# A scheduled DeltaNet + SwiGLU kernel: a planner that counts TensorE's instruction packets, weight buffers let go one by one, and a new order

## The chip, the cores and the metric

The kernel runs on one core of one Trainium2 chip. The metric is device time in microseconds (us) of one execution. Before the change three runs took 669.87, 666.66 and 668.11 us (median 668.11). A separate execution was profiled; it took 668.94 us.

## The reference

Two blocks follow each other. DeltaNet runs over 4 batches x 8 heads x 768 steps with head dimension 48; its output, rearranged to 3072 tokens of 384 values, goes through an RMS norm and a SwiGLU feed-forward with 1536 hidden columns. All in float32.

```python
k_n = k / (np.linalg.norm(k, axis=-1, keepdims=True) + 1e-06)
for t in range(S):
    kt, vt, bt = (k_n[:, :, t], v[:, :, t], beta[:, :, t, None])
    y[:, :, t] = np.einsum('bhd,bhde->bhe', q[:, :, t], state)
    v_old = np.einsum('bhde,bhd->bhe', state, kt)
    state = state + bt[:, :, :, None] * np.einsum('bhd,bhe->bhde', kt, vt - v_old)
...
x = np.ascontiguousarray(attn_out.transpose(0, 2, 1, 3)).reshape(B * S, H * D)
...
rms = np.sqrt(np.mean(x * x, axis=-1, keepdims=True) + 1e-06)
xn = x / rms * rms_g
g = xn @ w_gate
silu = g * (1.0 / (1.0 + np.exp(-g)))
val = xn @ w_val
return (silu * val @ w_out).astype(np.float32)
```

## The kernel before

**Tiling.** The 768 steps are cut into 12 chunks of 64. For each chunk, `prep` makes the triangular inverse that turns the step-by-step recurrence into matmuls (chunks 0 and 1 by `invert`, the others by a sequence of VectorE or GpSimd operations and DMAs), `qpart` makes the masked scores, `recur` applies the state, makes the chunk's output, normalizes it and updates the state, and `ffn` or `ffn_plain` runs the feed-forward of the chunk's 256 tokens. Chunks 0 and 1 use `ffn_plain`: `up` (line 1331, six matmul instructions for each side, gate or value, of a 128-column block) and `down_mm` (L1313). The other chunks use a scheme with fewer products: `ffn` (L1426) and `down` (L1483).

**Small matmuls.** The recurrence uses matmuls of 64 rows and columns or less, 64 instructions and 64 weight loads an operation: L563 (scores), L675, L782 and L801 (`invert`), L1037 and L1052 (on the state), L1100, L1114, L1134, L1171 (`recur`). They follow each other far more densely than those of the feed-forward. L1259 transposes the normalized output of a chunk, and L1264, L1268 scale it into the feed-forward's input x. Filler matmuls (L1594) pad TensorE's waits in the start-up.

**The order.** Every operation is first put on a list by `P.add`, with its engine, an estimated duration, keys that it reads and writes, PSUM groups that it takes and gives back, and `size`, the number of instructions that it puts on TensorE's stream (a float32 matmul is two weight loads and two matmul instructions). There are 2,790. `Plan.run` decodes the string `ORDER`, two characters an operation, into one order of all of them; each engine's queue is that order restricted to the engine (SP's queue issues most DMAs). `Plan.times` walks the order and gives each operation a planned start. The planned starts are not used as times on the chip; they decide which PSUM bank a group gets (the one that by plan is free first) and where and how many filler matmuls are put, up to 110 us by plan. In `times`, TensorE's instruction fetch is modelled as a backlog: a store that fills at a constant rate (`FETCH`, `AHEAD`).

**Weights and the hold.** The weight matrices arrive as 18 transfers of 768 KB (64-bit numbers, converted on the chip). `weights` issues them from SP into seven `raw` buffers, and each is converted by two ScalarE and two VectorE operations (L475, L476, L470, L473). The first four go out at once. `hold` (line 490) makes the buffers raw[4], raw[5] and raw[6] wait: one tiny GpSimd copy into each reads `u_`, chunk 0's result of L1145, so that their transfers start only then. On SP's queue a transfer that waits keeps back all that follow it.

**The start-up.** The k of chunk 0 comes in two halves, one issued by SP, one by ScalarE. TensorE transposes it (`turn`, L540), ScalarE squares it (L584), VectorE sums (L585, L587), GpSimd takes the root (L589), VectorE goes on (L592 and the following). Then `invert` for chunk 0 is a serial chain, followed by `recur(0)` up to x at L1268, and the feed-forward of chunk 0 begins. `betas` (L643) needs two small loads of beta.

Of the kernel before, what the change touches and what calls it, by code (L numbers as in the profile page):

```python
# [9 lines left out]
FP32 = mybir.dt.float32  # L10
# [6 lines left out]
C = 64  # L17
W = 32
# [3 lines left out]
FETCH, AHEAD = 67.0, 120.0  # L22
EARLY, FETCH0, AHEAD0 = 130.0, 50.0, 150.0
# [9 lines left out]
    "#.#'#&#3#)#4###,#-#(#/#*#0#T#C#`#W#>#^#a#_#w#U#X#k#Y#$#Z#d#l#b#n#m#o#c#H#t#V#e#+#u#f#[#]#q#v#x#s#R#y#S#@#z#M#p#{#1#|"  # L33
    "#?#2#}#E#i#~#j$C$#${$$#r$'$($%$&$)$*#N$D$/#J$.#D$+$0$1$,$H#I%$$E#=$2$F$-%)#K$7$5#L$3$8$6$<#O#h#A$=$>$;$4$9#P$G$?%V$:"
    "#g$I$B#F$L$K$J$i$l$O$N$M#B$P$Q$R&2%Y$[$S$@#G$T$]%W%Z$^$V$k$j$U$_$v%X$f$q%e$`$a$W$m$b$Y%[$c$d#Q$X$Z$e$n$o&Q$A&E%]%`%^"
    "$|&F$p%a$~$w&I%_&G%b$x&H&J$y$s%3%c$r&M%d$g%.&K$t&N$h&3&L$z#5&R&O%f$}$u'2%g%+&4&P%h'3%%%#&S'4&+%i%&&,&T%j%*%=%k&X%8%l"
    "&U%/%B%,&Y&V(4%1%m(5&^%n&Z%0#8&_&-#7&[%q%G%r%o%2&W%4%s%p&]&`%x%5%6%y%L&.#:%t%z%C#<&/&a%{%u%7&0%v%-%D'-%w%}%~%|%'%(&c"
    "&#&1%:#%&5&d'Q%H'0%9&b&?%E%?%Q%F'T'a%J'R&''.%I'1&&&@%K&$&('S&7%;&)'U&%#6'/%>'V&*&e%@'5%A'W'X%<'8%R'Y&h':'[%T%S&f'Z'9"
    "(6&i']%U&8'7%M&6&m'6&j(7%N&g(8'^)-#9).(<'K(9&k):#;';);%O&r'<%P'_&s&9'=)/'?&n)0'>(:'L&l)n'M&o&t&p'b&u&q'@'`'N)q'A'c)o"
    "'B&:&w'P)r'd'e)p'O'f'C&v'g'h'G'i)s'j&x&A)u'k*P'H&|&C&y'l'D'E'F)t&{'m'I'J)y&z&})w'n&B)v'o'$&~*Q'#)x'p'%&D'q(;(I'r's'&"  # L40
# [75 lines left out]
class Plan:  # L116
# [90 lines left out]
    def run(self, free, filler=None, until=0.0):  # L207
# [1422 lines left out]
```

## Time and profile before

| | us |
|---|---|
| median of three runs | 668.11 (666.66 to 669.87) |
| the profiled execution, its time | 668.94 |
| the profiled execution, its span | 667.2 |
| ScalarE busy | 295.7 |
| GpSimd busy | 133.7 |

How to read what follows: times are us from the span's start. A row of the timeline has the start, the length, the engine, the line, the instruction, what it writes and reads, the shapes, a count, and in brackets the idle time before it and what ended it ("issue" means that nothing visible was waited for). PE is TensorE's matmuls, PEld its weight loads, DVE VectorE, ACT ScalarE, POOL GpSimd, SP SyncE; a q behind the name is the engine's queue issuing a DMA. In a view of stretches, each row has the stretch, its length, then for PE, PEld, DVE, ACT and POOL the busy time and the number of instructions, then the granted TensorE clock, the DMA engines' busy share and GB/s.

### The profile page before, as it was taken

The page shows a single profiled execution, that of the slowest core. Times are in us where ns is not written, and L with a number is a line of the kernel's source. Part 1 is how long each engine was busy: PE and PEld are TensorE (multiplying, and loading weights), DVE is VectorE, ACT ScalarE, POOL GpSimd, SP SyncE. Part 2 cuts the span into 40 slices and gives each one's busy share as a digit, 9 for nine tenths or more (in the row PEclk, how much of TensorE's full clock was granted, in tenths as well). Part 3 has the DMA queues.
Part 4 walks back from the last instruction along what each step waited for, and adds up shares of the span by engine and source line. Part 5 has one row for each costly group of instructions (what it writes and reads, how often), then busy time and mean ns, then how long its engine had stood idle before and what let it go on. Part 6 is the DMA issues. An engine that isn't in the chain of part 4 may idle for free.

```text
span 667.2 us, 23209 instructions
## 1 busy us (share of the span) xinstructions
PE 654.4 (98%) x9934; PEld 604.8 (91%) x9934; DVE 543.3 (81%) x1147; ACT 295.7 (44%) x705; POOL 133.7 (20%) x204
## 2 busy tenths in 40 slices
PE   9999999999999999999999999999999999999997
PEld 5687887887799999999999999999999999999997
DVE  5879799888898798799888898799898799557463
ACT  4677553235336435454445345344445244263240
POOL 2210423021610410520410410420410301000000
PEclk9999899999999999999999999999999999999999
DMA  9959754666465566376375565666355333300101
GB/s 213 239 157 269 203 140 72 109 160 103 64 113 78 118 106 127 68 136 102 68 126 98 88 113 108 111 114 114 73 98 103 74 63 67 63 31 20 25 1 25
DMA packets 270423, 69.36 MB, mean 104 GB/s; under 512 B 257456, under 2 KB 262576, under 8 KB 270000
## 3 DMA queue, kind: packets, MB, share of 16 engines
q1 hardware_dynamic: 269280, 67.68, 51.1%
q8 instruction: 78, 1.28, 0.8%
q10 hardware_dynamic: 1040, 0.20, 0.2%
q14 instruction: 25, 0.20, 0.1%
HBM read 49.76 MB, written 22.02 MB: 108 GB/s over the span
## 4 chain that ended last, share of the span: by engine, by line
PE 91%; DVE 3%; issue 2%; POOL 2%; SPq 1%; DMA 1%; ACT 0%; POOLq 0%; ACTq 0%
PE bank L1426 40%; PE bank L1483 19%; PE bank L1331 8%; PE bank L1313 4%; PE bank L563 3%; PE bank L1037 3%; PE bank L1594 3%; PE bank L1114 2%; PE bank L1100 1%; PE bank L782 1%; PE bank L801 1%; PE bank L1171 1%; PE bank L979 1%; PE bank L999 1%; SPq L377 1%
## 5 line engine op out<-in xcount | busy, mean ns | idle before, releaser
L1426 PE MATMUL bank<-xf,w_in 128*128 128x128 f32 x1440 | 178.8, 276 | 0.3 <-DVE tmp L1436 0.3
L1426 PEld LDWEIGHTS bank<-xf,w_in 128*128 128x128 f32 x1440 | 169.3, 192 | 1.8 <-DVE tmp L1436 0.5
L1436 DVE TENSOR_TENSOR tmp<-tmp,bank 128x512 f32<-128x512 f32 x180 | 120.1, 682 | 46.9 <-PE bank L1426 28.9
L1426 PE MATMUL bank<-xf,more 128*128 128x128 f32 x960 | 122.8, 276 | 0.1
L1426 PEld LDWEIGHTS bank<-xf,more 128*128 128x128 f32 x960 | 114.9, 192 | 1.3 <-DVE tmp L1436 0.3
L1438 ACT COPY tmp<-bank 128x512 f32<-128x512 f32 x120 | 68.5, 587 | 99.9 <-PE bank L1426 78.5
L930 DVE TENSOR_REDUCE acc<-acc 128x30 f32<-128x90 f32 (+4 forms) x150 | 71.0, 473 | 5.2
L1442 ACT ACTIVATE tmp<-tmp 128x256 f32<-128x256 f32 x120 | 47.6, 415 | 61.9 <-DVE tmp L1436 61.8
L1483 PE MATMUL bank<-wo_sb,hf 128*128 128x192 f32 x360 | 64.0, 329 | 0.0
L1483 PEld LDWEIGHTS bank<-wo_sb,hf 128*128 128x128 f32 x360 | 58.0, 190 | 1.1 <-issue 0.4
L924 DVE TENSOR_TENSOR acc<-acc,at 128x60 f32<-128x60 f32 (+4 forms) x150 | 52.9, 353 | 5.9 <-POOL at L904 2.8
L1443 DVE TENSOR_TENSOR hf<-tmp 128x256 f32<-128x256 f32 x120 | 47.7, 418 | 3.0 <-ACT tmp L1442 2.2
L608 POOL TENSOR_TENSOR knrm<-ksum,half 128x16 f32<-128x16 f32 x11 | 32.0, 2913 | 85.2 <-DVE ksum L587 85.1
L869 POOL TENSOR_TENSOR at<-at,beta_b 128x256 f32<-128x256 f32 (+3 forms) x32 | 18.0, 593 | 149.0 <-DMA at<-dkk 149.0
L1313 PE MATMUL bank<-wo_sb,hf 128*128 128x384 f32 x96 | 33.8, 488 | 1.1 <-issue 1.1
L1331 PE MATMUL bank<-xp,w_in 128*128 128x256 f32 x144 | 34.7, 397 | 0.1
L1331 PE MATMUL bank<-xf,w_in 128*128 128x256 f32 x144 | 33.0, 382 | 0.0
L1331 PEld LDWEIGHTS bank<-xp,w_in 128*128 128x128 f32 x144 | 28.0, 198 | 4.5 <-DVE hf L1340 0.2
L1283 DVE TENSOR_TENSOR xf<-xf 128x256 f32<-128x256 f32 (+1 forms) x70 | 27.5, 432 | 5.2 <-ACT xf L1253 2.6
L1331 PEld LDWEIGHTS bank<-xf,w_in 128*128 128x128 f32 x144 | 26.9, 190 | 4.5
L950 POOL COPY acc<-acc 128x128 f32<-128x128 f32 x40 | 16.3, 438 | 71.4 <-DVE acc L930 70.7
L1313 PEld LDWEIGHTS bank<-wo_sb,hf 128*128 128x128 f32 x96 | 17.8, 190 | 10.3 <-issue 1.3
(207 smaller groups left out, 989.4 us busy)
## 6 DMA issues: line engine op xcount, KB each, us to landing
at<-dkk SPq DMA_DIRECT2D x20, 256.0 KB, 4.3
vt<-in_v_dram SPq DMA_DIRECT2D x24, 192.0 KB, 4.4
out_dram<-tmp SPq DMA_DIRECT2D x48, 96.0 KB, 2.2
k<-in_k_dram SPq DMA_DIRECT2D x23, 192.0 KB, 4.7
dks<-k SPq DMA_DIRECT2D x14, 256.0 KB, 4.0
kt<-dks SPq DMA_DIRECT2D x28, 128.0 KB, 3.8
more<-in_moe_w_gate_dram SPq DMA_DIRECT2D x4, 768.0 KB
more<-in_moe_w_out_dram SPq DMA_DIRECT2D x4, 768.0 KB
```

What stands on the lines that cost most here:

```text
L608: P.add("POOL", 2.95, lambda: nc.gpsimd.tensor_tensor(out=knrm[i2], in0=ksum[i2], in1=half, op=ALU.pow), pn, r=[("ksum", i2), "half"], w=[ ...
L924: nc.vector.tensor_tensor(out=acc[:, 1:3, 0:n, j + 2 : W].rearrange("p a i t -> p i a t"), in0=acc[:, old, 0:n, j : j + 2, None].to_broadc ...
L930: nc.vector.tensor_reduce(out=acc[:, new, 0:n, j + 2 : W], in_=acc[:, lo : lo + 3, 0:n, j + 2 : W].rearrange("p a i t -> p i t a"), axis=A ...
L1283: P.add("DVE", V(128 * n), lambda dst=dst, a=a, b_=b_, op=op: nc.vector.tensor_tensor(out=dst, in0=a, in1=b_, op=op), pxv, r=[("xp", 0), ( ...
L1313: nc.tensor.matmul(po[p].t[:, 0:DM], hf[:, spot(f), 128 * p : 128 * p + 128], wo_sb[:, spot(f)], start=(f == f0), stop=(f == f1 - 1), skip ...
L1331: nc.tensor.matmul(ps.t[:, TOK * side : TOK * side + TOK], w_in[:, side, h_, 3 * t + i_, n : n + 128], x_[:, 2 * t : 2 * t + 2].rearrange( ...
L1426: nc.tensor.matmul(g.t[:, 128 * z : 128 * z + 128], fac[:, side, 128 * f : 128 * f + 128], xf[:, xs], start=(begin and z == 0), stop=False ...
L1436: P.add("DVE", V(512), lambda t=t, g=g: nc.vector.tensor_tensor(out=t, in0=t, in1=g.t, op=ALU.add), -1, r=[g], w=[tk], last=g)
L1438: P.add("ACT", A(512), lambda t=t, g=g: nc.scalar.copy(t, g.t), -1, r=[g], w=[tk], last=g)
L1442: P.add("ACT", A(256), lambda t=t: nc.scalar.activation(out=t[:, 0:256], in_=t[:, 0:256], func=ACTF.Silu), -1, w=[tk])
L1443: P.add("DVE", V(256), lambda t=t, f0=f0, p=p: nc.vector.tensor_tensor(out=hf[:, spot(f0) : spot(f0) + 2, 128 * p : 128 * p + 128], in0=t[ ...
L1483: nc.tensor.matmul(g.t[:, 0:192], a_[:, f], b_[:, f], start=(begin and f == 0), stop=(f == 5), skip_group_check=True)
```

## The change

Three edits. First, `Plan.times` no longer models a backlog but packets: a packet of instructions is asked for whenever the count of instructions passes `PACKET[0] + PACKET[1] * n`, is there after `LAG[0]` plus a share of the DMA server's backlog, and TensorE waits for it when the count reaches its need, `PACKET[2]` instructions after the asking. The number of fillers is now worked out there too (`op.fill`), and `run` uses it. Second, `hold` has three different reads: raw[4] still waits for `u_`, raw[5] for the first tile of chunk 0's mean square and root (`ms[0]`), raw[6] for chunk 0's x (`xp1`). Third, `ORDER` is another permutation of the same 2,790 operations; it differs from the first line of the string to nearly the last. No computing operation is added or taken away.

```diff
-FETCH, AHEAD = 67.0, 120.0
-EARLY, FETCH0, AHEAD0 = 130.0, 50.0, 150.0
+PACKET = (130.2, 254.45, 314.0)
+LAG = (4.2, 0.55, 7.0)
...
 ORDER = (
-    "#.#'#&#3#)#4###,#-#(#/#*#0#T#C#`#W#>#^#a#_#w#U#X#k#Y#$#Z#d#l#b#n#m#o#c#H#t#V#e#+#u#f#[#]#q#v#x#s#R#y#S#@#z#M#p#{#1#|"
...
+    "#.#'#-###3#)#4#&#(#$#/#*#0#>#`#W#C#^#a#T#_#X#k#2#,#w#Y#b#Z#l#d#n#m#c#o#U#t#e#H#V#f#u#+#[#]#v#E#x#s#y#z#M#?#{#j#q#|#1"
...
-        server, self.end, mode, backlog, lands = 0.0, 0.0, 0, 0.0, []
+        server, self.end, mode, lands = 0.0, 0.0, 0, []
+        first, each, reach = PACKET
+        count, asked, used, there, pe = 0, 0, 0, {}, 0.0
+        lag = lambda t: LAG[0] + LAG[1] * min(max(server - t, 0.0), LAG[2])
...
-                rate, store = (FETCH, AHEAD) if s > EARLY else (FETCH0, AHEAD0)
-                fill = 6.0 if s < until else 0.0
-                backlog = max(0.0, backlog - (rate - fill) * (s - at["PE"])) + op.size - rate * op.dur
-                late = max(0.0, backlog - store) / rate
-                backlog, end = max(0.0, backlog - rate * late), end + late
+                op.fill = []
+                if s < until and any(x == SPARE and s < SPARE or x <= pe for x in free):
+                    op.fill = fillers(pe, s)
+                pe = s + op.dur
+                count += 4 * len(op.fill)
+                while first + each * asked <= count:
+                    there[asked] = s + lag(s)
+                    asked += 1
+                more, late, long = count + op.size, 0.0, end - s
+                while True:
+                    a, b = first + each * asked, first + each * used + reach
+                    if a >= more and b >= more:
+                        break
+                    if a <= b:
+                        t = s + late + (long * (a - count) / op.size if op.size else 0.0)
+                        there[asked] = t + lag(t)
+                        asked += 1
+                    else:
+                        t = s + late + (long * (b - count) / op.size if b > count else 0.0)
+                        if used < asked and there[used] > t:
+                            late += there[used] - t
+                        used += 1
+                count, end = more, end + late
...
-                if s < until and spare:
-                    filler(fillers(pe, s), spare[-1][1])
+                if op.fill:
+                    filler(op.fill, spare[-1][1])
...
     def hold():
-        for n in range(HELD, 7):
-            t = raw[n].bitcast(FP32)[:, 0:1]
-            P.add("POOL", 0.15, lambda t=t: nc.gpsimd.tensor_copy(out=t, in_=u_[:, 0, 0:1]), 29, r=[("u", 0, 0)], w=[("raw", n)])
+        for n, t, key in ((HELD, u_[:, 0], ("u", 0, 0)), (HELD + 1, ms[0][:, 0], ("ms", 0, 0)), (HELD + 2, xp1[:, 0], ("x1", 0))):
+            out_, in_ = raw[n].bitcast(FP32)[:, 0:1], t[:, 0:1]
+            P.add("POOL", 0.15, lambda out_=out_, in_=in_: nc.gpsimd.tensor_copy(out=out_, in_=in_), 29, r=[key], w=[("raw", n)])
```

94 lines of the change are left out of this document (47 added, 47 removed).

## Prediction

> **What bounds the kernel now.** I read the profile's page first (busy time, the span in slices, the chain of waits, the DMA queues).
>
> ```profile
> span 667.2 us, 23209 instructions
> PE 654.4 (98%) x9934; PEld 604.8 (91%) x9934; DVE 543.3 (81%) x1147; ACT 295.7 (44%) x705; POOL 133.7 (20%) x204
> PE   9999999999999999999999999999999999999997
> q8 instruction: 78, 1.28, 0.8%
> PE 91%; DVE 3%; issue 2%; POOL 2%; SPq 1%; DMA 1%; ACT 0%; POOLq 0%; ACTq 0%
> ```
>
> TensorE is busy in every slice and carries 91% of the chain that ends last. The change adds and removes no matmul of the computation, so it can win only two things: a TensorE start that comes earlier, and holes in its stream. The timeline of TensorE splits the span.
>
> ```profile
> 1.42 4.42 PE L1594 MATMUL bank<-ident 128*128 128x512 f32 x6 [1.42 <-POOL ident masks.py:199]
> 7.18 1.04 PE L540 MATMUL bank<-ident,k 128*128 128x128 f32 x8
> 23.66 2.06 PE L782 MATMUL bank<-mt,m1bd 64*64 64x32 f32 x64
> 44.33 0.27 PE L675 MATMUL bank<-kt 64*64 64x64 f32 x1 [0.93 <-issue]
> 44.53 8.04 PE L1331 MATMUL bank<-xp,w_in 128*128 128x256 f32 x36
> ```
>
> Up to 44.53 a serial start-up runs (filler matmuls of line 1594 pad it); from 44.53 on real work is packed, 622.7 us of it. The page shows 2% "issue" in the chain: time in which TensorE waited for nothing visible. I looked for where, listing the stalls and counting instructions up to each (stretches from zero; the x after PE and PEld are matmuls and weight loads), and then two stretches around one stall.
>
> ```profile
> 0.00:29.14 29.14, 27.72 (x350) 18.24 (x350) 20.70 (x64) 16.18 (x40) 6.13 (x11) 1.00 0.93 217
> 0.00:35.10 35.10, 32.98 (x476) 22.79 (x476) 25.30 (x75) 18.41 (x44) 8.82 (x12) 1.00 0.87 215
> 0.00:43.40 43.40, 40.62 (x731) 29.65 (x731) 29.73 (x86) 23.79 (x62) 11.59 (x19) 1.00 0.82 208
> 0.00:71.15 71.15, 67.28 (x1113) 52.03 (x1114) 55.74 (x146) 44.07 (x98) 14.48 (x20) 1.00 0.84 213
> 0.00:84.80 84.80, 79.69 (x1367) 62.77 (x1368) 65.75 (x165) 53.18 (x111) 18.98 (x25) 0.98 0.80 213
> 0.00:171.20 171.20, 165.39 (x2636) 131.12 (x2637) 143.22 (x323) 87.68 (x201) 39.17 (x47) 0.99 0.72 167
> 0.00:265.60 265.60, 258.75 (x4165) 219.58 (x4165) 223.97 (x492) 129.51 (x301) 62.28 (x84) 0.99 0.65 142
> 70.33:73.75 3.42, 2.11 (x100) 2.04 (x94) 3.32 (x9) 1.46 (x2) 0.84 (x1) 1.00 0.46 88
> 73.75:77.17 3.42, 3.42 (x11) 2.75 (x10) 2.31 (x5) 2.56 (x4) 3.13 (x3) 0.50 1.02 390
> ```
>
> Adding both columns, the stalls stand at instruction 700, 952, 1462, 2227, 2735, 5273 and 8330. The steps are 252, 510, 765, 508, 2538 and 3057: 1, 2, 3, 2, 10 and 12 times about 254.5. And 19,868 TensorE instructions by 78 packets of queue 8 are 254.7 a packet. So these holes are TensorE waiting for its next packet of instructions. The diff's constants say the same: with a packet asked for at 130.2 + 254.45 n and needed 314 later, the needs fall at 699, 953, 1462, 2225, 2734, 5279, 8332, within 6 of my counts.
>
> **Part 1, the packets.** The rows of the stalls, what one of them did to the clock (12 matmuls at 73.80 beside 12 normal ones), the two small groups ahead of it, and the largest stall for data:
>
> ```profile
> 29.77 0.41 PE L782 MATMUL bank<-mt,m1bd 64*64 64x32 f32 x6 [0.63 <-issue]
> 66.51 2.06 PE L782 MATMUL bank<-mt,m1bd 64*64 64x32 f32 x64
> 68.39 1.97 PE L801 MATMUL bank<-kk,x2bd 64*64 64x32 f32 x61
> 72.39 0.50 PE L1052 MATMUL bank<-state,kt 48*64 48x48 f32 x20 [1.31 <-issue]
> 73.80 4.50 PE L1331 MATMUL bank<-xp,w_in 128*128 128x256 f32 x12
> 84.90 1.19 PEld L1134 LDWEIGHTS bank<-r,mt 64*64 64x64 f32 x38 [0.23 <-issue]
> 103.08 0.62 PE L1259 MATMUL bank<-ident,yn 128*128 128x128 f32 x3 [0.57 <-ACT yn L1241]
> 106.35 2.86 PE L1331 MATMUL bank<-xp,w_in 128*128 128x256 f32 x12
> 172.24 2.74 PE L1313 MATMUL bank<-wo_sb,hf 128*128 128x384 f32 x8 [1.06 <-issue]
> 266.26 0.30 PE L999 MATMUL bank<-x2bd,kk 128*32 128x128 f32 x1 [0.67 <-issue]
> ```
>
> After 44.53 the packet stalls cost 1.31 + 0.23 + 1.06 + 0.67 = 3.27. The stretch with the 1.31 stall is busy 2.11 of 3.42, and in the next one the granted clock is 0.50: 12 matmuls take 4.50 instead of 2.86, another 1.64. Together **4.91 us** hang on packets.
>
> Does the new order remove them? I decoded both ORDER strings (two characters an operation) and added up instructions. Between asking and need lie 314 instructions, 157 matmuls. At the 71 us stall these are 41 of line 1052, all 64 of L801 and 52 of L782, the densest kind (64 in about 1 us): from 66.8 to 71.08, 4.2 us, and the packet came 1.31 later, after 5.5. With the median spacing of each kind the other stalled intervals are 3.8 (need 4.0) and 3.7 (need 4.4); the one at 171 is 6.9 and needed nearly 8, the DMA engines being loaded. In the new order the same boundary has three operations of L1331 (18 matmuls, 3.9 us at the 1.3 for six that 106.35 shows) among the small ones and lasts 7.3; the others become 5.6, 5.0 and 6.6. The shortest after the start are 5.0, 5.0, 5.3 and 5.4, where today they are 3.7, 3.8, 4.0 and 4.6. Today eleven intervals between 4.6 and 6.3 passed without a stall. So the 4.91 go; the 6.6 one, and any that meets a full DMA, may stall again. Bounds: 0 to 4.91 given back; I take 0.6, half of one stall of today's size, nearest to those eleven intervals without one. The diff does not show how many filler matmuls the new plan puts into the start-up (its times set that, and the banks); I keep today's. Twelve instructions fewer would make the shortest interval 4.1 (the one that stalls at 265 today), twelve more leave it at 5.0.
>
> [...]
>
> **Part 2, the start.** SP's and the other queues' first rows:
>
> ```profile
> 0.79 1.64 SPq L377 DMA_DIRECT2D tmp<-in_beta_dram  x2
> 2.47 0.67 SPq L377 DMA_DIRECT2D k<-in_k_dram  x1
> 6.39 0.84 ACT L584 ACTIVATE r<-k 128x768 f32<-128x768 f32 x1 [3.34 <-DMA k<-in_k_dram]
> 9.13 0.92 DVE L585 TENSOR_REDUCE ksum<-r 128x16 f32<-128x768 f32 x1
> 10.34 3.02 POOL L589 TENSOR_TENSOR knrm<-ksum,half 128x16 f32<-128x16 f32 x1 [8.97 <-DVE ksum L587]
> 13.74 0.21 DVE L592 TENSOR_SCALAR knrm<-knrm 128x16 f32<-128x16 f32 x1
> ```
>
> The new SP order issues k's half ahead of the two beta loads: 2.47 − 0.79 = 1.68 earlier. The betas move behind two transposes on TensorE. The first transposes then need not wait for k (landing about 6.39 − 1.68 = 4.7) but for the first fillers (end 1.42 + 4.42 = 5.84), so 7.3 becomes 5.84, 1.5 earlier. VectorE's reduce is put ahead of a memset, but still follows the copy out of those transposes, and its successors follow: 9.13 becomes about 7.0 to 7.9, the power on GpSimd starts about 9.3 and VectorE goes on at 12.3 instead of 13.74: **1.4 us** for the serial chain behind it. Bounds: 0 (an unmoved load, weights or v, ends last) to 1.68.
>
> At the end of the start-up:
>
> ```profile
> 38.59 1.19 POOL L1221 TENSOR_TENSOR rs<-ms,mhalf 128x1 f32<-128x1 f32 x1 [1.70 <-DVE ms L1214]
> 39.95 0.57 SPq L377 DMA_DIRECT2D wsum<-in_moe_w_val_dram  x1
> 41.82 0.92 ACT L475 ACTIVATE xf<-hf 128x768 f32<-128x768 f32 x1 [0.78 <-DMA hf<-in_moe_w_out_dram]
> 42.64 1.14 ACT L1268 ACTIVATE xp<-bank,g_sb 128x128 f32<-128x128 f32 x4
> 46.98 0.92 ACT L475 ACTIVATE xf<-wsum 128x768 f32<-128x768 f32 x1
> ```
>
> The weight conversion at 41.82 moves behind the four scalings of L1268, so x is ready about 1 us sooner than 43.78; the k scaling on GpSimd (L819) moves behind the first hold copy and fits into the 1.70 of idle time ahead of the root at 38.59. But the stall of 0.93 ends at 44.33, and the first feed-forward matmul is past instruction 1462: that packet, not x, opens the feed-forward. I credit 0.3 (bounds 0 and 0.93). The hold copies now wait for u, the first root and x, so the transfer issued at 39.95 and what is queued behind it on SP go at about 41 to 42, 1 to 2 us later. What it carries is first used by the eleventh feed-forward operation of TensorE, ten operations of about 1.3 us after the start, so not before 56. Today a transfer into that tile was in use 7 us after its issue (46.98), which makes 49, and the conversion is four operations of under 1 us on ScalarE and VectorE: some 3 us of cover are left, and I cost it at nothing. If that cover is gone, each us late is a us.
>
> **Part 3, the rest of the order.** By the decoded strings 1,870 of 2,790 operations stand at another place on their engine, after the start mostly swaps of near neighbours. The largest stall of TensorE for data is the 0.57 at 103.08; I take the new order's stalls for data as equal to the old one's. Bounds: 0.57 won, or 4 lost (seven such stalls).
>
> **Sum**, against the profiled execution's own 668.94: −4.91 + 0.6 − 1.4 − 0.3 = −6.0, so 662.9 (span 661.2). That execution lies 0.83 above the median of 668.11; −6.0 from the median is 662.1. I forecast **662.5**.
>
> **Rivals.**
> 1. *The stalls move.* Today's long wait (8 us) came with a loaded DMA; the new order's intervals are 5 to 7. Three such hits of 1.2 and one half-clock stretch of 1.64 return 5.2: 667. For: the 390 GB/s beside 73.75; against: eleven quiet intervals. Chance 0.17.
> 2. *The start does not move* (another load ends last), the stalls go: 668.11 − 4.3 = 663.8 or a little above. Chance 0.11.
> 3. *The holes are not fetches* but sit at those operations, and stay: only the start is won, 666.4. The counted steps of 254.5 speak against it. Chance 0.04. [...]
> 4. *Slower: x of chunk 1 comes late.* The old order has seven feed-forward operations of chunk 0 between the first transposition of L1259 (103.08) and the first of chunk 1, about 1.3 us each; the new one has three, and places the transposition 4.7 us of TensorE work later, so TensorE arrives at the same absolute time with less in reserve. On GpSimd two memsets, 1.0 and 0.7 us by the plan's durations, now stand ahead of the root that releases it. Being d late costs d, and beyond about 1.3 us also a half-clock 1.64. It is slower than now from d = 4.0, and by over 0.5% from 7.3: d = 9 gives 662.5 + 9 + 1.64 = 673. For: VectorE has 81% to do and the 0.57 wait there already; against: 1.7 on GpSimd is all I can count. Chance 0.10.
>
> **Numbers.** Forecast 0.58, rivals 0.17, 0.11, 0.04, 0.10. A measurement here can tell about 0.5%, 3.3 us, from nothing. Faster by that (under 664.8): 0.57 of the forecast's chance and about half of rival 2: 0.63. Same: rivals 1 and 3, the rest of 2, and a little of 4's small end: 0.28. Slower: 0.09. Range 659.5 (all 4.91, start 1.68 + 0.93, the 0.57, and 0.5 for runs that differ) to 668.5 (rivals 1 and 3 inside).
>
> **What would show it.** Right: no stall ended by "issue" at 60 to 90, 171 and 265; granted clock 1.00 from 60 to 80; first L540 near 5.9; line 1331 starting at 42.5 to 43.3; the last TensorE work some 6 us earlier. Wrong: "issue" stalls at other multiples of 254.5 (rival 1), L1331 still at 44.5 (rival 2), idle TensorE of some us ahead of L1259 near 102 with a half clock after it (rival 4).

## The result, and the profile after

The changed kernel takes 665.38 us in the median of 9 runs (664.39 to 667.44), the kernel before 668.11 in as many on the same chip (665.57 to 670.58): a ratio of 0.9957 with a 95% interval of 0.9938 to 0.9976. It is faster by 2.7 us; forecast were 5.6. Line numbers of the changed kernel are those of before plus 21 (L1331 is now L1352, L540 L561, L782 L803, L801 L822, L675 L696, L1134 L1155, L1313 L1334, L475 and L476 L496 and L497, L473 L494, L793 L814).

From the page of the changed kernel: its span, the engines' busy time and the chain that ended last.

```profile
span 663.7 us, 23214 instructions
PE 651.1 (98%) x9922; PEld 601.6 (91%) x9922; DVE 545.8 (82%) x1147; ACT 296.7 (45%) x705; POOL 135.0 (20%) x204
PE 66%; SPq 3%; DVE 2%; DMA 1%; issue 1%; ACT 1%; DVEq 0%; ACTq 0%
```

The span is 3.5 shorter (667.2 to 663.7). There are 12 matmul records fewer, and all of them are start-up fillers: the trace shows 40 on L1615 where 52 stood on L1594. Next TensorE's timeline of the changed kernel, the rows that answer to those shown of before (start, time from there to the end of the group, what it is, and in brackets the idle time ahead of it and what ended it):

```profile
5.65 1.06 PE L561 MATMUL bank<-ident,k 128*128 128x128 f32 x8
21.95 2.06 PE L803 MATMUL bank<-mt,m1bd 64*64 64x32 f32 x64 [0.34 <-DVE mt L782]
40.56 5.45 PE L1352 MATMUL bank<-xp,w_in 128*128 128x256 f32 x24 [0.41 <-ACT xp L1289]
48.60 1.13 PE L1352 MATMUL bank<-xp,w_in 128*128 128x256 f32 x4 [0.87 <-DVE w_in L494]
75.64 1.06 PE L561 MATMUL bank<-ident,k 128*128 128x128 f32 x8 [2.48 <-issue]
84.42 1.25 PE L1155 MATMUL bank<-r,mt 64*64 64x48 f32 x36 [1.08 <-issue]
```

Read against before: the feed-forward opens at 40.56 instead of 44.53, 3.97 earlier. It is opened by x now (L1289), not by a packet. The stalls at 171 and 265 are gone. But between 47 and 85 new ones stand: 0.87, 2.48 and 1.08 us. Two of them are ended by "issue", as the packet stalls of before were. Counting instructions up to each, and looking at the clock behind the first, in stretches of the changed kernel (PE busy and matmuls, PEld busy and weight loads, VectorE, ScalarE, GpSimd, granted clock, DMA share, GB/s):

```profile
0.00:73.17 73.17, 69.14 (x1200) 53.76 (x1200) 59.48 (x154) 46.22 (x100) 16.84 (x22) 1.00 0.90 224
0.00:83.50 83.50, 76.84 (x1368) 59.84 (x1368) 67.08 (x167) 53.83 (x112) 20.61 (x26) 0.98 0.84 216
73.43:76.84 3.41, 1.20 (x9) 1.13 (x10) 1.77 (x5) 3.33 (x6) 0.83 (x1) 1.00 0.27 92
76.84:80.26 3.42, 3.42 (x30) 1.99 (x28) 2.94 (x5) 3.37 (x5) 1.08 (x1) 0.50 0.39 123
```

The stall at 83.1 stands at 1368 + 1368 = 2736 instructions: 444.2 + 9 x 254.45 = 2734, the need of packet 9. The one at 73.2 stands at 2400, some 80 short of the next need (2480): it is no packet. After it the granted clock is 0.50 for 3.42 us, which costs about 1.5: four matmuls of L1334 take 2.47, where the same four take 1.45 or 1.46 at full clock, and L822 takes 2.57 where it takes 2.06 in a run below.

What does the 2.48 us stall wait for? ScalarE's timeline of the changed kernel shows it:

```profile
73.51 0.89 ACT L496 ACTIVATE kk<-wsum 128x768 f32<-128x768 f32 x1 [1.00 <-DMA wsum<-in_moe_w_val_dram]
74.31 0.87 ACT L497 ACTIVATE tmp<-more 128x768 uint32<-128x768 uint32 x1
75.08 0.47 ACT L814 ACTIVATE kk<-bank,side 128x256 f32<-128x256 f32 x1
```

L561 starts at 75.64, 0.09 after the first L814 has let go of its PSUM bank (75.08 + 0.47). L814's own inputs came from TensorE's L803, done by 73.2; but in the new order it stands behind two weight conversions on ScalarE, and the first of these waits for a transfer that landed near 73.5. In the old order the first L814 (there L793) came ahead of it, as ScalarE's timeline of before shows:

```profile
73.91 0.47 ACT L793 ACTIVATE kk<-bank,side 128x256 f32<-128x256 f32 x1 [2.12 <-PE bank L782]
75.89 0.90 ACT L475 ACTIVATE kk<-wsum 128x768 f32<-128x768 f32 x1 [0.71 <-DMA wsum<-in_moe_w_val_dram]
```

So the account of the span is: start 3.97 won; the packet stalls and the half clock behind them 4.91 won; lost 0.87 + 2.48 + 1.5 + 1.08 = 5.9; and 0.5 won over the rest makes the 3.5. (The wait of 0.57 for yn at 103 in before is gone too: nothing stands ahead of L1280, the line of L1259, in the changed kernel.) This is the account of one profiled execution of each kernel; a second pair follows below.

### The profile page after: what moved, and what is told of

Read it like the earlier page. It is cut to its first block, busy times and chain, and to the rows that moved or that the text cites. A ratio compares the mean times of both kernels' runs of the same rounds, so it can differ in the third digit from the quotient of the medians.

```text
span 663.7 us, 23214 instructions
## 1 busy us (share of the span) xinstructions
PE 651.1 (98%) x9922; PEld 601.6 (91%) x9922; DVE 545.8 (82%) x1147; ACT 296.7 (45%) x705; POOL 135.0 (20%) x204
## 4 chain that ended last, share of the span: by engine, by line
PE 66%; SPq 3%; DVE 2%; DMA 1%; issue 1%; ACT 1%; DVEq 0%; ACTq 0%
PE bank L1447 38%; PE bank L1504 19%; SPq L398 3%; PE bank L1058 2%; PE bank L584 2%; PE bank L1121 1%; PE bank L1135 1%; PE bank L1192 1%; DMA out_dram<-tmp 1%; PE bank L1000 1%; PE bank L1020 1%; DVE xf L1304 1%; DVE tmp L1457 0%; DMA k<-in_k_dram 0%; DVE acc L945 0%
## 5 line engine op out<-in xcount | busy, mean ns | idle before, releaser
L1464 DVE TENSOR_TENSOR hf<-tmp 128x256 f32<-128x256 f32 x120 | 47.7, 418 | 5.7 <-ACT tmp L1463 5.2
L1334 PE MATMUL bank<-wo_sb,hf 128*128 128x384 f32 x96 | 35.2, 501 | 0.0
L1352 PE MATMUL bank<-xp,w_in 128*128 128x256 f32 x144 | 33.5, 383 | 1.3 <-DVE w_in L494 0.9
L1352 PE MATMUL bank<-xf,w_in 128*128 128x256 f32 x144 | 33.2, 383 | 0.0
L1352 PEld LDWEIGHTS bank<-xp,w_in 128*128 128x128 f32 x144 | 26.8, 190 | 6.2 <-DVE w_in L494 1.3
L1304 DVE TENSOR_TENSOR xf<-xf 128x256 f32<-128x256 f32 (+1 forms) x70 | 29.1, 451 | 3.7 <-ACT xf L1274 2.0
L1352 PEld LDWEIGHTS bank<-xf,w_in 128*128 128x128 f32 x144 | 26.9, 190 | 4.7 <-DVE acc L945 0.2
L1334 PEld LDWEIGHTS bank<-wo_sb,hf 128*128 128x128 f32 x96 | 17.8, 193 | 8.9 <-issue 0.5
```

What stands on the lines that cost most here:

```text
L1304: P.add("DVE", V(128 * n), lambda dst=dst, a=a, b_=b_, op=op: nc.vector.tensor_tensor(out=dst, in0=a, in1=b_, op=op), pxv, r=[("xp", 0), ( ...
L1334: nc.tensor.matmul(po[p].t[:, 0:DM], hf[:, spot(f), 128 * p : 128 * p + 128], wo_sb[:, spot(f)], start=(f == f0), stop=(f == f1 - 1), skip ...
L1352: nc.tensor.matmul(ps.t[:, TOK * side : TOK * side + TOK], w_in[:, side, h_, 3 * t + i_, n : n + 128], x_[:, 2 * t : 2 * t + 2].rearrange( ...
L1464: P.add("DVE", V(256), lambda t=t, f0=f0, p=p: nc.vector.tensor_tensor(out=hf[:, spot(f0) : spot(f0) + 2, 128 * p : 128 * p + 128], in0=t[ ...
```

## The experiments

Twelve runs followed, in four groups; the ratio is to the kernel before, run beside them on the same chip. Before alone had medians of 666.39, 666.67, 667.93 and 667.30 in these four, so times are compared inside a group. One number is used throughout that no view prints: from the trace's records of the instruction queue I took when each packet landed, and called it asked for when TensorE reached 130.2 + 254.45 n instructions. That point, and the 314 instructions from it to the need, are the change's own constants: no record shows the asking itself, only the landing and the place of the stall.

### What the 2.48 us stall is: e1_wx_first

```diff
+MOVES = [([219, 215, 217], 278)]
...
+        for group, anchor in MOVES:
+            moved = [self.ops[i] for i in group]
+            order = [op for op in order if op not in moved]
+            k = order.index(self.ops[anchor]) + 1
+            order[k:k] = moved
```

219 and 215 are the two conversions, 217 VectorE's half of the second, 278 the second L814.

> The changed kernel with one move on ScalarE: the two scalings of L814 (round n = 1 of the inverse of chunk 1) stand ahead of the two weight conversions that stood in front of them; banks and fillers as in the changed kernel. Theory B (the 2.48 us hole at 73.17 is a PSUM bank that L814 still holds, queued behind a conversion that waits for its transfer): the hole shrinks to at most 0.6 us, and the half-clock stretch behind it goes (1.7); time 661.5 to 663.5, ratio to before 0.990 to 0.993. Rival P (it is an instruction packet, as the holes of before were): the hole stays at 2.5 us and the time at 665.4. Rival Q (the hole goes, but TensorE then waits for the same late weight a little later): hole under 0.6, time within 0.5 of 665.4.

Measured: 665.22 us, ratio 0.9979 (0.9955 to 1.0003). TensorE's timeline of this run:

```profile
73.49 1.09 PE L561 MATMUL bank<-ident,k 128*128 128x128 f32 x8
77.71 1.96 PE L822 MATMUL bank<-kk,x2bd 64*64 64x32 f32 x61 [1.83 <-DVE x2bd L797]
83.07 1.31 PE L1155 MATMUL bank<-r,mt 64*64 64x48 f32 x36 [0.25 <-issue]
```

ScalarE's, the first L814:

```profile
72.67 0.47 ACT L814 ACTIVATE kk<-bank,side 128x256 f32<-128x256 f32 x1
```

The hole is gone: L561 follows L803 at once. One swap on ScalarE took it away with every instruction, bank and filler of TensorE unchanged, so it was the bank (theory B), and P falls. But most of its worth did not come out: L822 now waits 1.83 for VectorE's L797, which stands behind the L494 whose input this very swap made later, and a stretch of lowered clock follows again (granted 0.73 from 78 to 82). In part that is Q: the next late thing stood two operations behind the first.

### Is the hold worth anything: e2_old_hold

```diff
-        for n, t, key in ((HELD, u_[:, 0], ("u", 0, 0)), (HELD + 1, ms[0][:, 0], ("ms", 0, 0)), (HELD + 2, xp1[:, 0], ("x1", 0))):
...
+        for n in range(HELD, 7):
...
```

> The changed kernel with the old hold: all three copies wait for u alone. Theory H0 (prediction: the hold is worth nothing): every time as in the changed kernel, 665.4, L1352 starting at 40.6. Theory H1 (the later transfers are what leaves the DMA engines free for the packets of the start-up): packet requests of the start-up last 5 to 6 us again, issue stalls of 0.5 to 0.9 come back before 40, L1352 starts at 42 to 43 and the time is 667 to 668. Theory H2 (the hold makes weights late): the 0.87 us wait of L1352 for L494 at 47.7 goes, time 664.5.

Measured: 664.96, ratio 0.9973 (0.9952 to 0.9993). TensorE's timeline:

```profile
41.42 4.80 PE L1352 MATMUL bank<-xp,w_in 128*128 128x256 f32 x21 [0.41 <-ACT xp L1289]
49.47 0.70 PE L1352 MATMUL bank<-xp,w_in 128*128 128x256 f32 x2 [0.88 <-DVE w_in L494]
```

No packet stall comes back in the start-up and the weight wait of 0.88 stays, so H1 and H2 fall; the hold is worth nothing that these runs can see. (The changed kernel did not run in this group; its ratios in two others are 0.9957 and 0.9979.)

### What the start's gain comes from: e4, e3, e5

e4 puts the first k load back behind the betas in the changed kernel. e3 puts it ahead of them in the kernel before, and the beta transposes (L643) behind the first turns (L540); e5 does only the latter. In the ORDER string these are moves of one or two pairs of characters; e4 and e5:

```diff
-    "#.#'#-###3#)#4#&#( ...
+    "#.#'###3#)#4#-#&#( ...
...
-    "#.#'#&#3#)#4###,#-#(#/#*#0#T#C#`#W#>#^#a# ...
+    "#.#'#&#3#)#4###,#-#(#/#*#0#C#`#W#>#^#T#a# ...
```

> The changed kernel with the first k load back behind the two beta loads on SP, nothing else moved. Theory S (the load sets the start): first L561 at about 7.0 instead of 5.65, L803 at 23.3 instead of 21.95, L1352 at 41.9 instead of 40.6, time 666.8. Rival F (the chain is set elsewhere, or its slack eats the delay): L561 later, but L1352 within 0.4 of 40.6, time 665.4.

> The kernel before with the first k load ahead of the two beta loads on SP and the beta transposes behind the first turns on TensorE, nothing else. Theory S (prediction): L540 at 5.8, L782 at 22.2 instead of 23.66, L1331 at 43.1 instead of 44.5, time 666.7, the three issue stalls of the start-up still there (1.76 in sum). Rival W (the earlier start alone also removes the packet stalls of the start-up): L1331 at 40.6 to 41.5, time 664 to 665.

> The kernel before with only the two beta transposes (L643) behind the first turns on TensorE; the k load stays behind the beta loads. Theory T (what held the first turns was their place behind L643 and the fillers put around it, and the load is worth only what the run with k behind the betas lost, 0.3 to 0.6): L540 at 6.2 to 6.4, L782 at 22.7 to 23.0, L1331 at 41.6 to 42.1, time as of the kernel with both. Rival L (prediction: the load is the gain): L540 at 7.0 or later, L1331 at 44, time of the kernel before.

Measured: e4 665.44, ratio 0.9984 (0.9957 to 1.0010); e3 664.63, 0.9972 (0.9946 to 0.9999); e5 664.88, 0.9980 (0.9960 to 1.0000). TensorE's timeline of e4:

```profile
6.26 1.06 PE L561 MATMUL bank<-ident,k 128*128 128x128 f32 x8 [0.65 <-DMA k<-in_k_dram]
41.15 5.02 PE L1352 MATMUL bank<-xp,w_in 128*128 128x256 f32 x22 [0.41 <-ACT xp L1289]
83.25 1.95 PE L1155 MATMUL bank<-r,mt 64*64 64x48 f32 x36 [2.21 <-issue]
```

Of e3, with the packet stall ahead of L1052:

```profile
5.95 1.48 PE L540 MATMUL bank<-ident,k 128*128 128x128 f32 x8
22.48 2.06 PE L782 MATMUL bank<-mt,m1bd 64*64 64x32 f32 x64
41.41 4.80 PE L1331 MATMUL bank<-xp,w_in 128*128 128x256 f32 x21 [0.15 <-ACT xp L1268]
70.62 0.38 PE L1052 MATMUL bank<-state,kt 48*64 48x48 f32 x11 [2.11 <-issue]
```

Of e5:

```profile
6.44 1.37 PE L540 MATMUL bank<-ident,k 128*128 128x128 f32 x8 [0.39 <-DMA k<-in_k_dram]
22.86 2.06 PE L782 MATMUL bank<-mt,m1bd 64*64 64x32 f32 x64
41.91 4.37 PE L1331 MATMUL bank<-xp,w_in 128*128 128x256 f32 x19 [0.15 <-ACT xp L1268]
```

e5 moves one operation of the old kernel and has the feed-forward open at 41.91 instead of 44.53. The load adds 0.5 to that (e3, 41.41), and taking it out of the changed kernel costs 0.6 (e4, 41.15) against its first profile and nothing against its second (41.16, below). In before, ScalarE could read k at 6.39 and L540 ran at 7.18: it stood behind L643, which waits for the betas, and behind six fillers (5.99) that the planner put after that. Theory T holds, S and L fall; F's bound of 0.4 is kept against the second profile alone.

The move brings a second thing. With ten filler matmuls fewer (42 for 52), the span from L782 to L1331 is 19.05 in e5 instead of 20.87: of the three packet stalls of the start-up (0.63, 0.20, 0.93) one of 0.33 is left in e5, at 33.9, and none that the timeline prints in e3, since the needs lie 20 instructions further on in the work and the third falls into L1331 itself. So W was right for e3.

These two kernels have the old order everywhere else, the old planner and the old hold, and their times stand to before as the changed kernel's do (next run). So at this precision the rest of the change wins nothing on balance. Their stall ahead of L1052 is larger, not smaller (2.11 and 2.20).

### Both kernels once more: after_again, before_again

> The changed kernel once more, for a second profile of it and its time beside the others on one chip. Every theory expects the wait of L561 near 73 again (1.3 to 2.5 us, ended by the first L814 of ScalarE), the weight wait of L1352 near 47.5 (0.9), an issue stall of L1155 near 81 to 83 at instruction 2734, none near 171 and 265; L1352 starting between 40.5 and 41.5.

> The kernel before once more, for a second profile. Theory N (holes are packets that are late, and how late depends on the run's transfers): issue stalls at the counts 699, 953, 1462, 2225 and 2734 again, of other sizes than 0.63, 0.20, 0.93, 1.31, 0.23; those at 171 and 265 may be missing, as they were in two other kernels with nearly this order. Rival O: the same seven stalls with the same sizes within 0.1.

after_again: 664.95, ratio 0.9979 (0.9962 to 0.9996). before_again had one run, 669.76, beside a median of 667.93. TensorE's timeline of after_again:

```profile
41.16 5.02 PE L1352 MATMUL bank<-xp,w_in 128*128 128x256 f32 x22 [0.41 <-ACT xp L1289]
74.93 1.81 PE L561 MATMUL bank<-ident,k 128*128 128x128 f32 x8 [1.11 <-POOL r L1083]
83.56 1.25 PE L1155 MATMUL bank<-r,mt 64*64 64x48 f32 x36 [0.85 <-issue]
```

And of before_again:

```profile
44.04 2.21 PE L1331 MATMUL bank<-xp,w_in 128*128 128x256 f32 x9
71.62 0.59 PE L1052 MATMUL bank<-state,kt 48*64 48x48 f32 x20 [1.03 <-issue]
172.76 1.45 PE L1313 MATMUL bank<-wo_sb,hf 128*128 128x384 f32 x4 [0.78 <-issue]
266.80 0.30 PE L999 MATMUL bank<-x2bd,kk 128*32 128x128 f32 x1 [0.65 <-issue]
```

The bank wait is there again, smaller (the profile puts it down to GpSimd's L1083, but the first L814 ends at 74.83, 0.10 ahead of L561), and so are the weight wait and the packet stall. In before the stalls at 71, 171 and 265 came again with 1.03, 0.78 and 0.65 (1.31, 1.06 and 0.67 in the first profile), and the first two of the start-up did not come at all. So a packet stall keeps its place, and its size belongs to the execution: N rather than O, though the one at 265 is as O has it. Between these two profiles, taken on different chips, the feed-forward opens 2.88 earlier (44.04 to 41.16) instead of 3.97.

### Packets or operations: e6_finer_fillers

```diff
-        for w_ in n:
+        for w_ in [x for y in n for x in ((2, 1, 1) if y == 4 else (y,))]:
```

> The changed kernel with each start-up filler of 512 columns issued as 256 + 128 + 128: the same columns, 104 more TensorE instructions before the first L803, nothing else. Theory N (packets: a need at 444.2 + 254.45 n counted instructions, usable 1.3 us after it landed): the need of packet 9 moves from L1155 (83) back into L584, 9 us after its request, and the stall of 1.1 to 1.3 us ahead of L1155 goes; the need of packet 8 moves into L803 near 72.6, only 3.6 us after its request, and an issue stall of 2 to 3.5 us stands inside L803, which the bank wait of L561 behind it mostly covers (L561 still starts when the first L814 ends). Time 0.5 to 1.5 below the changed kernel. Rival O (the holes belong to the operations): the stall ahead of L1155 stays, none inside L803, time as of the changed kernel.

TensorE's timeline of this run:

```profile
75.40 0.53 PE L803 MATMUL bank<-mt,m1bd 64*64 64x32 f32 x10 [2.26 <-issue]
82.66 2.02 PE L1155 MATMUL bank<-r,mt 64*64 64x48 f32 x64
```

And the count up to the stall:

```profile
0.00:73.17 73.17, 69.21 (x1242) 60.14 (x1242) 60.15 (x154) 47.01 (x101) 16.85 (x23) 1.00 0.91 228
```

Forecast to the place: a stall inside L803, at 1242 + 1242 = 2484 instructions (need of packet 8: 2480), and none ahead of L1155, whose 64 matmuls run in one piece. No data changed, only how many instructions the idle time of the start-up is cut into. This shows the packets. The time went the wrong way, though: 667.29, ratio 1.0012 (0.9992 to 1.0031), 2.3 above the changed kernel in the same group, while its profiled execution (665.64) was its second best. That other needs now fall where 314 instructions are short (in this profile stalls ended by "issue" also stand at 39.7, 0.53, and at 361.7, 0.50) is likely, but not shown.

### Taking the waits out: c1_reordered, c2_reordered, c3_no_middle_fillers, s1_old_order_aligned

c1 to c3 are the changed kernel with the operations of ScalarE and VectorE that TensorE waits for put ahead of weight conversions, and two operations of L1352 put where packet 9 needs time. VectorE's and TensorE's order around 75, by line:

```
VectorE   changed  L494 L797 L797 L1080 L491 L491 L494 L828 L1361 L828
          c1       L797 L797 L1080 L494 L491 L491 L494 L828 L1361 L828
          c2, c3   L797 L797 L494 L1080 L491 L828 L1361 L828 L654 L491 L494
TensorE   changed  L561 L1334 L822 L822 L584 L1155 L1155 L1352 L1352
          c1 to c3 L561 L1334 L822 L822 L584 L1352 L1352 L1155 L1155
```

s1 is e3 with 132 more instructions in the start-up, counted out so that the needs of packets 7 and 9 fall into slow stretches:

```diff
-        for w_ in n:
+        for w_ in n if n == [4, 4, 2] else [x for y in n for x in ((1, 1, 1, 1) if y == 4 else (y,))]:
```

> The changed kernel with what the runs so far point to: on ScalarE the two L814 and the two L573 behind them ahead of the weight conversions, on VectorE the two L797 and L1080 ahead of L494, on TensorE two operations of L1352 (1.3 us each) moved ahead of L1155, into the time that packet 9 needs, and L1058 ahead of the L1352 that waits for its weights at 47.7. Theory G (the holes of 47 to 85 are these waits, and nothing is right behind them): no stall over 0.4 us between 47 and 90, granted clock 1.00 throughout, L1352's work of chunks 0 and 1 done 4 to 6 us sooner, time 660 to 661.5 where the changed kernel has 665.4 (4 to 5.5 below it on this chip). Rival R (the next late thing takes it back: weights that are converted later, other banks): stalls of 2 us or more at new places before 110, time within 1.5 of the changed kernel.

> The changed kernel with the moves of c1 but for L1058, and with VectorE's two L828, L1361 and L654 put ahead of the weight conversions that L828 stood behind (3.08 us of L1352 in c1), and ScalarE's first L497 between the two L814. Theory G (queue positions behind conversions are the whole of it): no wait over 0.5 between 50 and 90, granted clock 1.00; L1155 of chunk 1 done at 83.0 to 83.6 with two operations of L1352 more ahead of it, that is 4 to 5 us gained on the changed kernel there; time 660.5 to 662 (0.991 to 0.994 of before). Rival R (the conversions pushed back are themselves awaited next): a wait of 1.5 us or more for L494 or L872 before 110, time within 1.5 of the changed kernel.

> c2 without the five fillers (ten matmuls, 3.2 us of TensorE) that the planner put at 78 us in c2, where its model expected L584 to wait; in c2 L584's inputs were there at 76.0. Theory G (the fillers alone ate what c2 had won): L584 starts at once behind L822, L1155 of chunk 1 is done at 83.5 to 84.5 instead of 87.2, no wait over 0.6 between 50 and 90, time 662 to 663 (0.990 to 0.993 of before on one chip), that is 2.5 to 3.5 below c2 and below the changed kernel. Rival R (something else is late there, a bank or packet 9, which is wanted 20 instructions and 3 us earlier): a stall of 2 us or more between 78 and 85, time as c2, 665.5.

> The old order, old planner and old hold of the kernel before, with the start of run e3 (k load ahead of the betas, beta transposes behind the first turns), and the eleven later start-up fillers of 512 columns issued as four of 128 each: 132 more TensorE instructions before the first L782, nothing else. Theory N (packets by instruction count): the need of packet 7 leaves L1052 (68.3 in run e3) and falls where 314 instructions last 7 us or more, that of packet 9 leaves L1134; no issue stall over 0.4 between 45 and 110, granted clock 1.00 there, L1331 within 0.6 of 41.4, its 144th matmul near 106 instead of 110.25, time 4 to 5 below run e3, that is 660 to 661 (0.990 to 0.992 of before). Rival O: the stall of 2.3 stays ahead of L1052 and the half clock behind it; time as run e3. Rival M (other packets become the late ones, as in the run with finer fillers): those two stalls go, but others of 0.5 to 1 each behind 110 take back 1.5 or more.

c1: 666.23, ratio 1.0000 (0.9981 to 1.0019). TensorE's timeline:

```profile
82.04 5.49 PE L1352 MATMUL bank<-xp,w_in 128*128 128x256 f32 x12 [3.08 <-DVE mt L828]
```

VectorE's timeline of c1 around it:

```profile
77.26 0.96 DVE L494 CUSTOM_DVE_ANT_0 w_in<-xf,tmp 128x1536 uint16<-128x1536 uint16 x1 [2.31 <-ACT tmp L497]
80.71 0.95 DVE L494 CUSTOM_DVE_ANT_0 w_in<-kk,tmp 128x1536 uint16<-128x1536 uint16 x1
81.57 0.41 DVE L828 TENSOR_TENSOR mt<-mt,bank 128x256 f32<-128x256 f32 x1
```

Rival R: the waits taken away came back as one of 3.08, again the wait for an engine whose queue stands behind conversions, and 12 matmuls at half clock behind it (5.49; 2.86 in c2).

c2: 665.49, ratio 0.9958 (0.9937 to 0.9979). TensorE's timeline, and behind it its busy time in a stretch:

```profile
76.13 2.06 PE L822 MATMUL bank<-kk,x2bd 64*64 64x32 f32 x64
78.12 3.29 PE L1615 MATMUL bank<-ident 128*128 128x512 f32 x10
81.33 1.16 PE L584 MATMUL bank<-kt 64*64 64x64 f32 x64
85.22 2.07 PE L1155 MATMUL bank<-r,mt 64*64 64x48 f32 x64
```

```profile
75.00:100.00 25.00, 24.61 (x394) 19.12 (x393) 20.37 (x36) 13.17 (x26) 7.86 (x7) 1.00 0.54 149
```

TensorE is busy for 24.61 of 25 us, at a granted clock of 1.00, and nothing is won: the planner, which recomputes its times for a new order, expected L584 to wait and put five fillers (3.2 us) ahead of it. L584's copies were ready at 76.0. An engine that is busy in every slice can be busy with nothing.

c3, without those five fillers: 663.42, ratio 0.9939 (0.9900 to 0.9978). TensorE's timeline:

```profile
77.58 1.12 PE L822 MATMUL bank<-kk,x2bd 64*64 64x32 f32 x33 [0.80 <-issue]
82.50 2.07 PE L1155 MATMUL bank<-r,mt 64*64 64x48 f32 x64
159.02 0.61 PE L1280 MATMUL bank<-ident,yn 128*128 128x128 f32 x3 [0.86 <-ACT yn L1262]
```

Its clock at the last of these:

```profile
156.00:159.50 3.50, 1.84 (x11) 1.22 (x10) 2.42 (x3) 2.36 (x5) 0.76 (x2) 1.00 0.04 6
159.50:163.00 3.50, 3.50 (x8) 1.85 (x7) 1.40 (x4) 2.88 (x8) 0.00 (x0) 0.54 0.58 90
```

L1155 is done at 84.57 instead of 87.29 in c2: most of theory G. It is the lowest median of all, 2.1 below c2 (in another group), with intervals that overlap. This execution gave its gain back at 156 to 163, where two waits of 0.8 and 0.86 for yn have another half-clock stretch behind them. Whether c3 beats the changed kernel is likely by the medians (0.9939 against 0.9957 and 0.9979), not settled.

s1: 665.80, ratio 0.9984 (0.9952 to 1.0015). TensorE's timeline:

```profile
224.78 0.81 PE L563 MATMUL bank<-qt,kt 64*64 64x64 f32 x26 [4.47 <-issue]
```

The stalls ahead of L1052 and L1134 went as counted. But a wait of 1.5 for ScalarE's L793 came in their place, with a granted clock of 0.50 from 79.0 to 82.5, 1.4 of waiting for x ahead of L1331, and in the profiled execution packet 26 landed 10.25 us after it was asked for: 4.47 in one stall (rival M). So neither theory's time came out.

## Why the prediction was right, and where it was wrong

**Direction and range** held: faster, 2.7 us where 5.6 were forecast. By the stated 0.5% the result (0.43%) counts as "same", which the text gave 0.28. Both sides of the sum, won and lost, were too small: the start won 2.3 more than its 1.7, and 5.9 were lost where 0.6 were set aside. That these errors in part cancel is luck. By the text's own signs it is mixed: the stalls at 171 and 265 went and L561 came near 5.9, but stalls ended by "issue" (2.48 and 1.08) and a granted clock of 0.50 stand between 60 and 90.

**Part 1, what goes: right for four of five terms.** Nothing stands at the need of packet 7 near 71, nothing at 171 and 265, in both profiles, and the 1.64 of half clock behind the first went with it; the fifth term, 0.23 at the need of packet 9, grew (next paragraph). The counting itself is shown by e6, where 104 instructions of filler moved a stall to the forecast place. But e3 and e5 say that the new order was not needed for all of it: with the old order and 20 filler instructions fewer, the stall at 171 went in both and the one at 265 in e3. In e5 one of 0.63 still stands at that need (instruction 8330, at 264.4), in L1483 instead of L999. The one at 71 stayed in both: that one the new order removed.

**Part 1, "I take 0.6" given back: mis-sized.** The packet at 83 cost 1.08, and 2.21 in e4. Interval and need were both off. The interval was forecast as 5.6, with today's fillers. It lasted 5.60, but by luck: the new plan puts 12 filler matmuls (24 instructions) fewer ahead of it, so the same count falls later, into denser work, and half clock stretched it again. In e4, which has the same TensorE stream and a granted clock of 1.00 there, it is the stretch from instruction 2422 to 2736:

```profile
76.49:80.83 4.34, 4.34 (x159) 3.79 (x157) 4.34 (x9) 3.58 (x7) 2.56 (x3) 1.00 0.65 209
```

That is 4.34. The text had priced fewer fillers only for the need at 265 (4.1); there 6.3 came out, and no stall. For the need it used the lag of the stalled packets of before (4.0 to 5.5, "nearly 8" for the one at 171, where the DMA share was 1.09 from 164.87 to 170.80) and leaned on eleven intervals of 4.6 to 6.3 without a stall. Packet 9 landed 5.5 after it was asked for, and TensorE went on 1.4 after that: 6.9 in all, nearer the upper than the lower end of what the stalls of before had shown (6.8 in e4, 5.7 in the second profile).

**Part 3, "stalls for data equal": the step that failed.** It counted TensorE's waits of before and took them for those of after. The new order puts the conversion that waits for a transfer ahead of the first L814 on ScalarE, and the PSUM bank that L814 holds is the one L561 wants: 2.48, and 1.5 of half clock behind it, which is the whole of the bound of 4 lost that the text kept but did not choose; with the 0.87 at 47.7 it is passed. A look at ScalarE's order around each operation that frees a bank would have found it: the operation ahead of it waits for a transfer. The 0.87 at 47.7 is a cousin: TensorE waits for a conversion, L494, that stands on VectorE behind operations of an inverse (L715 to L734); VectorE is busy there with hardly a gap (6.32 of 6.59 us from 41.00 to 47.59), and waits for no transfer. Rival 1 had nearly the right sum (5.2 back, measured 5.9) for the wrong reason: only 1.08 of it is a packet. Rival 2 falls with L1352 at 40.56, and rival 4 with L1280, ahead of which TensorE does not wait.

**Part 2, the start: right in size for what it named, wrong in its cause, and too small.** First L561 was forecast at 5.84 and came at 5.65 and 5.84; L803 1.4 earlier, measured 1.71 and 1.10. The text gave this to the load; e4 and e5 give it to L643 and its fillers, and 0.0 to 0.6 to the load. The further 2.3 (the same in both profiles) were bounded by "that packet, not x, opens the feed-forward", credited at 0.3: the packet came earlier too, and it was no longer needed first. With 24 filler instructions fewer the feed-forward opens at instruction 1440, ahead of the need at 1462. In the changed kernel packets 1 to 4 landed 2.2 to 3.2 us after they were asked for; in before it was 3.4 to 5.9. A term tied to "the packet" should have been followed through with the packets' new needs and times, as the same text did for the later ones in Part 1.

**The hold at nothing: right** (e2).

**Rival 3 falls:** stalls of 0.25 to 4.5 us stand at the counted needs in ten of the kernels, and move with the count.

## What to carry to other kernels

When a planner reorders, check each engine that *releases* something (a PSUM bank, a tile), not only the engine that sets the end: what stands ahead of the release, and does that wait for a transfer? Where TensorE's instruction stream is the limit, count instructions: here 104 filler instructions more in the start-up put a stall of 2.26 us at instruction 2484, near 73 (e6), and 20 fewer went with a stall of 2.11 and 2.20 instead of 1.31 near 71 and with none at 171 (e3, e5). And before a new order is credited with a gain, try the cheapest part alone: here one transpose operation moved behind another, with the ten filler matmuls that the planner then left out, had the whole of it, as far as these runs can tell (ratio 0.9980 beside 0.9957 and 0.9979).

## What the runs showed of the hardware

Between a packet's landing and TensorE's going on lay 1.2 to 1.6 us in the packet stalls from 68 to 85 of all these kernels and in the one of s1 (1.34 and 1.35 in before, 1.44 in the changed kernel). At 265 in before it was 2.1 and 1.9, longer than a packet alone accounts for elsewhere; what held TensorE there stays open. From asking, as defined above, to landing took 1.9 to 8.1 us in the first profiles of before and of the changed kernel, and over 10 twice in s1. The runs of a kernel spread differently: 9.0 us between the fastest and the slowest but one of s1's 12, 3.1 to 8.7 between fastest and slowest in most, and 1.1 in c2, in whose profile every packet from 40 to 190 landed at least 2.2 us ahead of its need. Whether late packets make the spread was not shown.

The half clock came once in each of the first two profiles: a granted clock of 0.50 for 3.42 us, from 73.75 in before and from 76.84 in the changed kernel. In the stretch of that length ahead of it TensorE was still busy for a third (1.20 of 3.41 in the changed kernel) or more than half (2.11 of 3.42 in before); in c3 it was 1.84 of 3.50, with two waits of 0.80 and 0.86 us, none as long as the "about 1.3" of rival 4, and 0.54 was granted in the 3.50 behind. Behind the single waits of 1.06 at 171 in before and of 1.08 at 83 in the changed kernel the clock stayed at 1.00.
